# Row maxima split into two float16 parts ahead of their transpose, in a two-layer sliding-window transformer kernel

## The chip, the cores and the metric

The kernel runs on one core of a Trainium2 chip. A core has five engines with a queue each, which work in order and wait for each other through semaphores: TensorE (PE in the profile; its weight loads are shown apart as PEld), VectorE (DVE), ScalarE (ACT), GpSimd (POOL) and SyncE (SP, which issues all DMAs here). The metric is the device time of one execution in microseconds (us), lower is better.

## The reference

Two identical layers over a sequence of 2048 rows of width 640. Each adds to x a causal attention with 32 heads of 20 columns, in which a query sees the 256 latest positions, and then a feed-forward block with a squared ReLU.

```python
def _A_ref(x, wqkv, wo):
    B, S, D = x.shape
    H = 32; Dh = D // H; W = 256
    qkv = (lambda x, *d: x.transpose(*d))((x @ wqkv).reshape(B, S, 3, H, Dh), 2, 0, 3, 1, 4)
    q, k, v = qkv[0], qkv[1], qkv[2]
    scores = jnp.einsum("bhqd,bhkd->bhqk", q, k) * (Dh ** -0.5)
    idx = jnp.arange(S)
    mask = (idx[:, None] - idx[None, :] >= 0) & (idx[:, None] - idx[None, :] < W)
    scores = jnp.where(mask[None, None], scores, -1e9)
    p = _softmax(scores, axis=-1)
    o = jnp.einsum("bhqk,bhkd->bhqd", p, v)
    return (lambda x, *d: x.transpose(*d))(o, 0, 2, 1, 3).reshape(B, S, D) @ wo
...
x = A_x
x = x + _A_ref(_layernorm(x, axis=-1), A_wqkv, A_wo)
x = x + _B_ref(_layernorm(x, axis=-1), B_w1, B_b1, B_w2, B_b2)
x = x + _A_ref(_layernorm(x, axis=-1), A_wqkv, A_wo)
x = x + _B_ref(_layernorm(x, axis=-1), B_w1, B_b1, B_w2, B_b2)
```

The softmax needs, for each query and head, a number near the largest score of its row, to keep the exponentials in range. The change touches how that number travels.

## The kernel before, in words

**Precision.** Dense products (queries, keys, values, output projection, both feed-forward products) are made of float16 halves: each operand is split into a high part and the rest, and three float16 matmuls replace one float32 matmul (function `mm3`, line 256).

**Units.** The sequence is cut into blocks of 256 rows; with two layers there are 16 units. In a unit the 32 heads are taken as 8 quads of four heads, and the quads as four groups G of two (`GQ` = 2). For each quad the program does three things:

- `max_quad`: scores with queries as rows (PE, line 523) into the PSUM tiles `bb`, then eight DVE instructions that add a mask and keep the maximum of each row (line 535; the profile shows each as a main instruction and a read of the accumulator into `mx`). `mx` holds, for one group, 128 partitions (queries) by 16 float32 columns (heads and halves).
- `exp_quad`: the scores once more, now with keys as rows (PE, line 585), the exponentials (ACT, line 598) and the masks (POOL, lines 613 and 617).
- `pv_quad`: exponentials times values (PE, line 647).

**How the maximum enters.** `exp_quad` multiplies 62 rows instead of 60: two extra rows of the query tile `qt` hold the negated row maximum as two float16 parts, and the key tile holds constants there. So the maxima of a group must be turned from a column per head into a row per head. That is `max_out`, once per group, 64 times in the program: a PE transpose of `mx` (line 547) into a PSUM tile `tr`, two DVE operations that make the two float16 parts in the SBUF tile `mT` (lines 552 and 553), and four DMAs that lay the parts into `qt` (line 560). The first `exp_quad` of the group needs them.

**What sets the order.** Each engine's instruction order is written out by the program while it is built. A small planner keeps a simulated time `now` and one clock per engine. PE work is emitted as the Python code reaches it; work for ACT, DVE, POOL and SP is posted as jobs with a cost and a priority (`post`), and `pump` puts a job into its engine's queue when the planner thinks it can start. `need(job)` moves `now` forward until the planner has put that job and believes it finished; it emits nothing on PE meanwhile. `mm_tile` hands out one of two PSUM banks in which dense products, transposes and `pv` results take turns. In units 1 to 15 `together` walks the quads: `exp_quad`, then `max_out` of a group whose maxima were made a turn before, a stretch of dense matmuls, the next `max_quad`, `pv_quad`, more dense matmuls. So a transpose stands in PE's queue right behind the 16 score matmuls of line 585 and ahead of dense matmuls of line 256. On DVE, the work that lies around it is what the planner thought due at that time: the last maxima (535), splits of queries and keys (414), of the feed-forward activations (826) and of layer-norm results (352), and the scaling of attention outputs by reciprocals (726, 729, 736).

Of the kernel before, what the change touches and what calls it, by code (L numbers as in the profile page):

```python
# [10 lines left out]
F32 = mybir.dt.float32  # L11
F16 = mybir.dt.float16
BF16 = mybir.dt.bfloat16
AF = mybir.ActivationFunctionType
ALU = mybir.AluOpType

P = 128
S = 2048
D = 640
# [18 lines left out]
MS = 2.0 ** 4  # L38
# [6 lines left out]
def kernel(ctx: ExitStack, tc: tile.TileContext, x, wqkv, wo, w1, b1, w2, b2, out):  # L45
    nc = tc.nc
# [3 lines left out]
    sb = ctx.enter_context(tc.tile_pool(name="sb", bufs=1))  # L50
    ps = ctx.enter_context(tc.tile_pool(name="ps", bufs=1, space=bass.MemoryType.PSUM))


    ident = sb.tile([P, P], F32, name="ident")
    make_identity(nc, ident)
    neghalf = sb.tile([P, 1], F32, name="neghalf")
    nc.vector.memset(neghalf, -0.5)
    maskb = sb.tile([P, 3 * P], BF16, name="maskb")
# [32 lines left out]
    now, clk, pend, moved = [0.0], {"A": 0.0, "D": 2e3, "G": 0.0, "S": 0.0}, [], [0.0]  # L91
# [28 lines left out]
    def post(eng, cost, fn, *deps, wait=0.0, prio=1, **kw):  # L120

        j = Job(eng, cost, fn, [d for d in deps if d is not None], now[0] + wait, prio, **kw)
        k = len(pend)
        while k and pend[k - 1].prio > prio:
            k -= 1
        pend.insert(k, j)
        return j

    def dma(fn, size, *deps, n=1, cost=450.0, prio=1, **kw):

        return post("S", n * cost, fn, *deps, prio=prio, size=size, **kw)
# [14 lines left out]
    def pass_time():  # L146
        now[0] = max(now[0], min(k.start() for k in pend if k.ready()) - LOOK)
        pump()

    def need(*js):  # L150

        for j in js:
            while j.end is None:
                pass_time()
            now[0] = max(now[0], j.end)
# [4 lines left out]

    banks2 = []

    def mm_tile(shape, name):


        while len(banks2) > 1:
            empty = [b for b in banks2 if b and all(j.end is not None for j in b)]
            if empty:
                b = min(empty, key=lambda b: max(j.end for j in b))
                now[0] = max(now[0], max(j.end for j in b) + LAT)  # L170
                banks2.remove(b)
            else:
                pass_time()
        t = ps.tile(shape, F32, name=name, tag="mm", bufs=2)
        banks2.append([])
        return t, banks2[-1]

# [112 lines left out]
    def split_t(y, dst, job, made, bb=None):  # L290


        need(job)
        for k, (c0, n) in enumerate(((0, 3), (3, 2))):
            if bb is not None:
                tr, jobs = bb[:, k].rearrange("p (c n) -> p c n", n=P), bbjobs
            else:
                tr, jobs = mm_tile([P, 4, P], "tr")
            for c in range(n):
                nc.tensor.transpose(tr[:, c, :], y[:, (c0 + c) * P:(c0 + c + 1) * P], ident)  # L300
            j = post("A", 170 * n, lambda tr=tr, c0=c0, n=n: nc.scalar.copy(dst[:, 0, c0:c0 + n], tr[:, :n]),
                     wait=117 * n, prio=0)
            j = post("D", 170 * n, lambda tr=tr, c0=c0, n=n:
                     nc.vector.tensor_sub(dst[:, 1, c0:c0 + n], tr[:, :n], dst[:, 0, c0:c0 + n]), j, prio=0)  # L304
            jobs.append(j)
            made.append(j)
            yield 117 * n
# [77 lines left out]
    def stage_qk(u, which=(0, 1)):  # L385
# [7 lines left out]
        for j, c0 in order:  # L393
# [11 lines left out]
            dst = kts[u % 3] if j else qts[u]  # L405
            n = min(2, KC - c0)
            acc, jobs = mm_tile([P, 2, T], "acc")
            s = QS / (YS * WS)

# [60 lines left out]
    def stage_v(u, which=range(4)):  # L470
        yT = yTs[u]
        for i in range(2):
            vt = vts[(2 * u + i) % 6][0]
            for h in range(2):
                if 2 * i + h not in which:
                    continue
                acc, jobs = mm_tile([P, 2 * T], "acc")
                need(*[wqj[c] for c in range((2 * D + h * HD) // P, (2 * D + (h + 1) * HD - 1) // P + 1)])
                def out(vt=vt, acc=acc, h=h):
                    nc.scalar.activation(vt[:, h * NP:(h + 1) * NP, 0:DH],  # L480
                                                 acc[:, :HD].rearrange("p (h d) -> p h d", d=DH),
                                                 AF.Copy, scale=1.0 / (YS * WS))

                yield from mm3(acc[:, :HD], lambda a, k: yT[:, a, k, i * P:(i + 1) * P],
                               lambda b, k: wq_s[:, b, k, 2 * D + h * HD:2 * D + (h + 1) * HD], KC, 136,
                               lambda wait: jobs.append(post("A", 320, out, wait=wait, prio=0)))


    GQ = NQ // 4
# [51 lines left out]
    def max_out(u, G):  # L541

        qt, mx = qts[u], mxs.pop((u, G))
        NR = 8 * GQ
        need(*mxjobs.pop((u, G)))
        tr, jobs = mm_tile([P, 4, P], "tr")
        nc.tensor.transpose(tr[:NR, 0, :], mx.rearrange("p e n i -> p (e n i)"), ident)  # L547
        now[0] += 220.0
        mT = sb.tile([NR, 2, P], F16, name="mT", bufs=1)

        def rows():
            nc.vector.tensor_scalar(mT[:, 0], tr[:NR, 0, :], -1.0 / MS, None, op0=ALU.mult)
            nc.vector.scalar_tensor_tensor(mT[:, 1], tr[:NR, 0, :], -1.0 / MS, mT[:, 0],
                                           op0=ALU.mult, op1=ALU.subtract)

        def spread():
            for e in range(2):
                for a in range(2):
                    r = 64 * e + 3 * DH + a
                    nc.sync.dma_start(qt[r:r + 1, 2 * GQ * G:2 * GQ * (G + 1), :].rearrange("p n (i m) -> p (n i) m", i=2),  # L560
                                      mT[4 * GQ * e:4 * GQ * (e + 1), a, :])

        j = post("D", 520, rows, prio=0)
        jobs.append(j)
        rowjobs[u, G] = dma(spread, 16384, j, n=4, cost=600.0, prio=0)

# [341 lines left out]
    def together(ns, ms, dense, cost, share=1.0, whole=True, after=None, pace=0):  # L908
# [5 lines left out]
        for k, (part_, what, m) in enumerate(ts):  # L914
            if what and what[0] == "s":
                quad = exp_quad(what[1])
                for it in late:
                    max_out(*it)
                late.clear()
            if m is not None:  # L920
                max_quad(m)
                if m % GQ == GQ - 1:
                    late.append((m // NQ, m % NQ // GQ))
            if what and what[0] == "v":
                pv_quad(what[1], quad)
            if after and k == 0:
                after()
            part += part_
            while done < cost * share * part / total:
                c = next(dense, None)  # L930
                if c is None:
                    break
                step(c)
                done += c
            if what is None:
                for it in late:
                    max_out(*it)
                late.clear()
# [5 lines left out]
    def flow(todo, dense):  # L944

        todo = list(todo)
        quad = None
        while todo:
            kind, n = todo[0]
            u, G = n // NQ, n % NQ // GQ  # L950
            wants = {"m": [*bbjobs, trips.get((u, 0, n % NQ)), trips.get((u, 1, n % NQ))], "r": mxjobs.get((u, G), [None]),
                     "s": [*bbjobs, *([rowjobs.get((u, G))] if n % GQ == 0 else [])],
                     "v": quad[1][0] if quad else []}[kind]
            if not all(j is not None and j.end is not None and j.end <= now[0] + LOOK for j in wants):
                c = next(dense, None)
                if c is not None:
                    used[0] += c
                    step(c)
                    continue
                need(*[j for j in wants if j is not None])  # L960
            todo.pop(0)
            if kind == "m":
                max_quad(n)
            elif kind == "r":
                max_out(u, G)
            elif kind == "s":
                quad = exp_quad(n)
            else:
                pv_quad(n, quad)
            pump()  # L970
# [29 lines left out]
    for u in range(1, NU):  # L1000
        last = u == NU - 1
        quads, ahead = range(NQ * u, NQ * (u + 1)), range(NQ * u + LEAD, NQ * (u + 1) + LEAD)
        parts, cost, ahead_ln = [], OC + FCST, None
# [49 lines left out]
```

## Time and profile before

| | |
|---|---|
| median of 3 runs | 1659.74 us (1657.5 to 1660.65) |
| span of the profiled execution | 1660.5 us; no other time is given for that execution |
| PE busy | 1595.4 us, 96% |
| DVE, ACT, POOL busy | 1032.8 us, 750.1 us, 636.8 us |
| mean granted TensorE clock | 0.986 |
| transposes of maxima (547) | 64, 280 ns mean each, from 47.8 us to 1553.8 us |
| `mT` operations (552, 553) | 64 each, 279 ns mean each |

How to read the rows. In a timeline a row begins with the start in us from the span's start and the duration; rows that follow each other with the same form are merged with their count; what stands in brackets is the idle time of the engine just before and who ended it. The printed duration of a DVE or PE instruction contains its latency, so the next one often begins a little before the printed end. On PE the starts of neighbouring matmuls tell more than their durations, since matmuls are pipelined. From about 250 us to 1400 us the program repeats itself, apart from the border of the layers near 820 us, with a period of 98.5 us, a unit (the transposes at 622.81 us and 721.27 us are one period apart).

### The profile page before, as it was taken

Reading aid. Unit: us, or ns where it says so; the run is one execution under the profiler, and the core shown is the slowest. Engines: PE = TensorE matmul, PEld = TensorE weight load, DVE = VectorE, ACT = ScalarE, POOL = GpSimd, SP = SyncE. Lnnn points to the kernel's source line nnn. Section 1 sums busy time; section 2 is a strip of 40 time slices with the busy share of each in tenths; the row PEclk is TensorE's granted clock in tenths of the full one; section 3 lists DMA queues with packets and bytes.
Section 4 is the critical chain, followed back from the end, with each engine's and each line's share of the span. In section 5 each row is a group of like instructions: output and inputs, shape, how many; then the busy total and the mean of one; then the engine's idle time right before and its main releaser. Section 6 shows DMA issues by size and latency. Waiting matters only on the chain.

```text
span 1660.5 us, 44547 instructions
## 1 busy us (share of the span) xinstructions
PE 1595.4 (96%) x17574; PEld 1173.0 (71%) x17574; DVE 1032.8 (62%) x3231; ACT 750.1 (45%) x1616; POOL 636.8 (38%) x1309
## 2 busy tenths in 40 slices
PE   7787899999999999999999999999999999999989
PEld 5564676777777777777777777777777777776667
DVE  7566657675665766566565756657665666757341
ACT  4455534535444454544434354444545444453512
POOL 1343533524344353424414243443534344353512
PEclk9897999999999999999999999999999999999999
DMA  8465214343452534335153433424343352421020
GB/s 245 129 179 155 61 61 107 63 118 84 100 101 60 125 69 113 78 102 118 50 136 74 123 82 104 98 68 118 73 109 80 104 115 50 108 70 53 26 64 17
DMA packets 231484, 157.42 MB, mean 95 GB/s; under 512 B 79468, under 2 KB 215020, under 8 KB 231276
## 3 DMA queue, kind: packets, MB, share of 16 engines
q1 hardware_dynamic: 231276, 154.59, 37.8%
q8 instruction: 138, 2.26, 0.6%
q14 instruction: 70, 0.57, 0.1%
HBM read 84.68 MB, written 52.95 MB: 83 GB/s over the span
## 4 chain that ended last, share of the span: by engine, by line
PE 87%; DVE 5%; ACT 3%; DMA 3%; issue 1%; SPq 1%; POOL 0%; DVEq 0%; ACTq 0%; POOLq 0%
PE acc L256 65%; PE pv L647 10%; PE bb L585 6%; PE bb L523 5%; DVE bb L535 2%; ACT pt L598 2%; DMA qk<-qd 1%; PE tr L547 1%; DMA qk<-yl 0%; DMA w_s<-in_A_wqkv_dram 0%; DVE mx L535 0%; DMA ov<-o 0%; DMA qt<-qk 0%; ACT r L816 0%; SPq L560 0%
## 5 line engine op out<-in xcount | busy, mean ns | idle before, releaser
L535 DVE CUSTOM_DVE_ANT_0 bb<-bb,maskb 128x384 f32<-128x384 f32 (+2 forms) x1024 | 510.4, 565 | 117.3 <-PE bb L523 109.4
L598 ACT ACTIVATE pt<-bb 128x512 f32<-128x512 f32 (+1 forms) x736 | 376.5, 602 | 239.9 <-PE bb L585 239.6
L613 POOL TENSOR_SCALAR_AFFINE_SELECT pt<-pt 128x256 f32<-128x256 f32 x448 | 195.0, 440 | 542.8 <-ACT pt L598 521.4
L256 PE MATMUL acc<-y,w_s 128*128 128x256 f16 x2880 | 331.8, 273 | 4.2 <-DVE y L304 1.4
L256 PE MATMUL acc<-w_s,hh 128*128 128x320 f16 x2304 | 326.2, 299 | 0.0
L256 PEld LDWEIGHTS <-w_s 128*128 128x128 f16 x2880 | 278.5, 98 | 58.2 <-issue 25.7
L256 PE MATMUL acc<-yT,wq_s 128*128 128x256 f16 x2400 | 282.7, 276 | 12.6 <-DVE qd L414 10.6
L256 PEld LDWEIGHTS <-hh 128*128 128x128 f16 x2304 | 221.8, 98 | 97.8 <-issue 15.3
L256 PEld LDWEIGHTS <-wq_s 128*128 128x128 f16 x2400 | 233.7, 99 | 58.0 <-issue 27.8
L617 POOL TENSOR_SCALAR_AFFINE_SELECT pt<-pt 128x256 f32<-128x256 f32 x512 | 217.1, 446 | 64.3 <-ACT pt L598 63.2
L826 DVE TENSOR_TENSOR hh<-r,hh 128x256 f16<-128x256 f32 x192 | 91.7, 499 | 208.4 <-ACT hh L823 200.9
L647 PE MATMUL pv<-pt,vt 128*32 128x128 f32 (+1 forms) x3840 | 188.8, 331 | 2.0 <-POOL pt L617 1.4
L820 POOL TENSOR_TENSOR r<-r 128x256 f32<-128x256 f32 x192 | 113.5, 612 | 184.9 <-ACT r L816 183.4
L659 ACT COPY ot<-pv 128x256 f32<-128x256 f32 x128 | 47.6, 372 | 285.6 <-PE pv L647 285.6
L535 DVE DVE_READ_ACCUMULATOR2_ANT mx<- 128x1 f32 x1024 | 142.7, 139 | 0.1
L256 PE MATMUL acc<-wq_s,yT 128*128 128x320 f16 x960 | 142.0, 301 | 0.1
L647 PEld LDWEIGHTS pv<-pt,vt 128*32 128x32 f32 x3840 | 104.2, 110 | 49.1 <-issue 17.6
L256 PE MATMUL acc<-wo_s,od 128*128 128x320 f16 x900 | 131.9, 301 | 3.6 <-DVE x L758 1.7
L816 ACT ACTIVATE r<-acc,b1s 128x256 f32<-128x256 f32 x192 | 80.6, 471 | 99.8 <-PE acc L256 98.4
L256 PEld LDWEIGHTS <-yT 128*128 128x128 f16 x960 | 93.0, 98 | 40.4 <-issue 7.0
L585 PE MATMUL bb<-qt,kt 62*128 62x128 f16 (+1 forms) x1920 | 109.4, 246 | 10.6 <-DVE mx L535 9.8
L256 PEld LDWEIGHTS <-od 128*128 128x128 f16 x900 | 86.1, 98 | 45.9 <-issue 11.1
(84 smaller groups left out, 1175.7 us busy)
## 6 DMA issues: line engine op xcount, KB each, us to landing
qt<-qk SPq DMA_DIRECT2D x30, 480.0 KB
kt<-qk SPq DMA_DIRECT2D x30, 480.0 KB
qk<-qd SPq DMA_DIRECT2D x17, 640.0 KB
o<-ot SPq DMA_DIRECT2D x256, 42.0 KB
od<-o SPq DMA_DIRECT2D x13, 640.0 KB
qk<-yl SPq DMA_DIRECT2D x13, 640.0 KB
qk<-qd SPq DMA_DIRECT2D x17, 320.0 KB
xt<-in_A_x_dram SPq DMA_DIRECT2D x16, 320.0 KB
```

Source lines behind the costliest of these rows:

```text
L256: nc.tensor.matmul(acc, lhs(a, c), rhs(b, c), start=(k == 0), stop=(k == 3 * nk - 1))
L523: nc.tensor.matmul(to, qt[r, p, i * P:(i + 1) * P], kt[r, p, a:b], start=True, stop=True)
L535: nc.vector.tensor_tensor_reduce(out=v, in0=v, in1=mask, scale=1.0, scalar=-3.0e38, op0=ALU.add, op1=ALU.max, accum_out=accum)))
L585: nc.tensor.matmul(bb[e][:, k, o:o + w], kt[r, 2 * qd + j, ko:ko + P], qt[r, 2 * qd + j, q0 * P:q0 * P + w], start=True, stop=True)
L598: nc.scalar.activation(box["pt"][:, :o], bb[e][:, k, :o], AF.Exp, scale=SCALE / (QS * QS))
L613: nc.gpsimd.affine_select(out=m, in_=m, pattern=[[0, 2], [-1, P]], compare_op=ALU.is_gt, fill=0.0, base=0, channel_multiplier=1)
L617: nc.gpsimd.affine_select(out=m, in_=m, pattern=[[0, 2], [1, P]], compare_op=ALU.is_ge, fill=0.0, base=0, channel_multiplier=-1)
L647: nc.tensor.matmul(pv[32 * jj:32 * (jj + 1), q0 * P:(q0 + qn) * P], vf[:, c:c + 32], pj[:, j, :], start=(k == 0), stop=(k == len(steps) - ...
L659: nc.scalar.copy(ot[:, qd % 2], pv)
L816: nc.scalar.activation(box["r"], acc[:, f, :], AF.Relu, bias=b1s[:, f0 + f:f0 + f + 1], scale=1.0 / (YS * WS))
L820: nc.gpsimd.tensor_tensor(box["r"], box["r"], box["r"], op=ALU.mult)
L826: nc.vector.tensor_sub(hh[:, 1, f, :], box["r"], hh[:, 0, f, :])
```

## The change

The two float16 parts are now made from `mx` itself, on 128 partitions by 16 columns, ahead of the transpose. Both parts lie side by side in a new float16 tile `mh` of 32 columns; one float16 transpose (with a float16 identity, made once at the start) turns all 32 columns into 32 rows, and one DVE copy takes them from PSUM to `mT`. The four DMAs are the same, with other source rows. The parts are posted as a DVE job, and the code waits for it with `need` ahead of the transpose.

```diff
@@ -53,6 +53,8 @@
     ident = sb.tile([P, P], F32, name="ident")
     make_identity(nc, ident)
+    ident16 = sb.tile([P, P], F16, name="ident16")
+    nc.vector.tensor_copy(ident16, ident)
...
-    def mm_tile(shape, name):
+    def mm_tile(shape, name, dtype=F32):
...
-        t = ps.tile(shape, F32, name=name, tag="mm", bufs=2)
+        t = ps.tile(shape, dtype, name=name, tag="mm", bufs=2)
...
         need(*mxjobs.pop((u, G)))
-        tr, jobs = mm_tile([P, 4, P], "tr")
-        nc.tensor.transpose(tr[:NR, 0, :], mx.rearrange("p e n i -> p (e n i)"), ident)
-        now[0] += 220.0
-        mT = sb.tile([NR, 2, P], F16, name="mT", bufs=1)
+        mh = sb.tile([P, 2, NR], F16, name="mh", bufs=1)
+        flat = mx.rearrange("p e n i -> p (e n i)")
+
+        def parts():
+            nc.vector.tensor_scalar(mh[:, 0], flat, -1.0 / MS, None, op0=ALU.mult)
+            nc.vector.scalar_tensor_tensor(mh[:, 1], flat, -1.0 / MS, mh[:, 0], op0=ALU.mult, op1=ALU.subtract)
+
+        need(post("D", 200, parts, prio=0))
+        tr, jobs = mm_tile([P, 8 * P], "tr", F16)
+        nc.tensor.transpose(tr[:2 * NR, :P], mh.rearrange("p a n -> p (a n)"), ident16)
+        now[0] += 60.0
+        mT = sb.tile([2 * NR, P], F16, name="mT", bufs=1)
 
         def rows():
-            nc.vector.tensor_scalar(mT[:, 0], tr[:NR, 0, :], -1.0 / MS, None, op0=ALU.mult)
-            nc.vector.scalar_tensor_tensor(mT[:, 1], tr[:NR, 0, :], -1.0 / MS, mT[:, 0],
-                                           op0=ALU.mult, op1=ALU.subtract)
+            nc.vector.tensor_copy(mT, tr[:2 * NR, :P])
...
-                                      mT[4 * GQ * e:4 * GQ * (e + 1), a, :])
+                                      mT[NR * a + 4 * GQ * e:NR * a + 4 * GQ * (e + 1), :])
...
-        j = post("D", 520, rows, prio=0)
+        j = post("D", 200, rows, prio=0)
```

Because jobs are put by the planner's clocks, the order on the engines moves a little too. The line numbers of the changed program are higher by 2 from line 56 on and by 8 behind `max_out` (354 there is 352 here, 416 is 414, 537 is 535, 737 is 729, 861 is 853).

The first place is on DVE, around the 29th of the 64 transposes (721 us in the profile before). Line 352 makes the low parts of a layer-norm result, line 853 adds a feed-forward product to x. Before:

```order
L535 ISA mx 128x1
L853 SCALAR_TENSOR_TENSOR x_9224<-acc,x_9224 128x320 [waits PE_49]
L352 TENSOR_TENSOR yl<-xt,yl 128x640 [waits Activation_49] x2
L552 TENSOR_SCALAR mT<-tr 16x128 [waits DMAHW4_49,DMAHW3_49,PE_49]
L553 SCALAR_TENSOR_TENSOR mT<-tr,mT 16x128 [waits DVE_49]
L853 SCALAR_TENSOR_TENSOR x_9225<-acc,x_9225 128x320 [waits PE_49]
```

In the changed program:

```order
L537 ISA mx 128x1
L861 SCALAR_TENSOR_TENSOR x_9276<-acc,x_9276 128x320 [waits PE_49]
L354 TENSOR_TENSOR yl<-xt,yl 128x640 [waits Activation_49] x2
L552 TENSOR_SCALAR mh<-mx 128x16 [waits DVE_49]
L553 SCALAR_TENSOR_TENSOR mh<-mx,mh 128x16 [waits DVE_49]
L562 COPY mT<-tr 32x128 [waits DMAHW4_49,DMAHW3_49,PE_49]
L861 SCALAR_TENSOR_TENSOR x_9277<-acc,x_9277 128x320 [waits PE_49]
```

The parts stand where the two `mT` operations stood, behind the same instructions, and the copy stands right behind them. On PE, at the same place, the transpose was one instruction and is now a weight load that waits for DVE, and a matmul:

```order
L593 LDWEIGHTS kt_79
L593 MATMUL bb<-qt,kt_79 128x256
L557 LDWEIGHTS mh [waits DVE_49]
L557 MATMUL tr<-ident_66,mh 32x128
L258 LDWEIGHTS hh
L258 MATMUL acc<-w_s,hh 128x320
```

It stands between the same neighbours as before, the last score matmul and the first dense one.

The second place is DVE around the next transpose (746 us before), where attention outputs are scaled: line 729 multiplies, 726 makes the reciprocals, 736 makes low parts. Before:

```order
L414 SCALAR_TENSOR_TENSOR qd<-acc,qd 128x256 [waits Activation_49]
L729 TENSOR_TENSOR od<-od,rs 128x5x64 [waits DMAHW1_49]
L726 RECIPROCAL rs<-rs 128x64
L552 TENSOR_SCALAR mT<-tr 16x128 [waits DMAHW7_49,DMAHW2_49,PE_49]
L553 SCALAR_TENSOR_TENSOR mT<-tr,mT 16x128 [waits DVE_49]
L736 TENSOR_TENSOR od<-od 128x5x64 [waits Activation_49]
```

In the changed program:

```order
L416 SCALAR_TENSOR_TENSOR qd<-acc,qd 128x256 [waits Activation_49]
L737 TENSOR_TENSOR od<-od,rs 128x5x64 [waits DMAHW1_49]
L552 TENSOR_SCALAR mh<-mx 128x16 [waits DVE_49]
L553 SCALAR_TENSOR_TENSOR mh<-mx,mh 128x16 [waits DVE_49]
L744 TENSOR_TENSOR od<-od 128x5x64 [waits Activation_49]
L562 COPY mT<-tr 32x128 [waits DMAHW7_49,DMAHW2_49,PE_49]
L734 RECIPROCAL rs<-rs 128x64
```

Here the parts have moved ahead of one reciprocal, which is now behind the copy.

The third place is in the first unit, around the 5th transpose (120 us before), where DVE also makes low parts of the feed-forward weights (line 196, 198 in the changed program). Before:

```order
L535 ISA mx 128x1
L196 SCALAR_TENSOR_TENSOR w_s<-w_s 128x5x128
L286 TENSOR_SCALAR xt<-xt,bmv 128x640 [waits Pool_49]
L552 TENSOR_SCALAR mT<-tr 16x128 [waits DMAHW6_49,DMAHW7_49,DMAHW0_49,PE_49]
L553 SCALAR_TENSOR_TENSOR mT<-tr,mT 16x128 [waits DVE_49]
```

In the changed program:

```order
L537 ISA mx 128x1
L198 SCALAR_TENSOR_TENSOR w_s<-w_s 128x5x128
L198 SCALAR_TENSOR_TENSOR w_s<-w_s 128x5x128 [waits DMAHW3_49,Activation_49]
L552 TENSOR_SCALAR mh<-mx 128x16 [waits DVE_49]
L553 SCALAR_TENSOR_TENSOR mh<-mx,mh 128x16 [waits DVE_49]
L562 COPY mT<-tr 32x128 [waits DMAHW6_49,DMAHW7_49,DMAHW0_49,PE_49]
L288 TENSOR_SCALAR xt<-xt,bmv 128x640 [waits Pool_49]
```

A second weight split, which stood later before, has come in ahead of the parts, and the layer-norm scaling of line 286 has gone behind the copy.

## The prediction

> **What bounds the kernel now.** I read the page's shares and its chain of waits first, then busy time by stage, then the rows of the transpose and its two followers, and last the timeline around single transposes.
>
> ```profile
> span 1660.5 us, 44547 instructions
> PE 87%; DVE 5%; ACT 3%; DMA 3%; issue 1%; SPq 1%; POOL 0%; DVEq 0%; ACTq 0%; POOLq 0%
> ```
>
> ```profile
> core 0: us, PE busy (x) PEld busy (x) DVE busy (x) ACT busy (x) POOL busy (x), PEclk, DMA share, GB/s
> 0.00:190.00 190.00, 147.28 (x1386) 103.50 (x1390) 120.51 (x391) 97.45 (x191) 63.14 (x107) 0.89 0.61 167
> 190.00:800.00 610.00, 606.07 (x6959) 450.37 (x6948) 393.84 (x1217) 282.06 (x612) 248.73 (x527) 1.00 0.38 89
> 1000.00:1400.00 400.00, 399.44 (x4586) 296.19 (x4582) 263.54 (x812) 183.74 (x395) 158.22 (x336) 1.00 0.39 93
> ```
>
> PE bounds it. In the first 190 us PE lacks 42.7 us of busy time; in the repeating stretches it lacks 3.9 of 610 us and 0.6 of 400 us. So a new wait of PE there has nothing to hide in: it lengthens the program by its full size. DVE, at 394 of 610 us, has room, but the question is when it is free, not how much it does.
>
> ```profile
> L547 PEld LDWEIGHTS tr<-ident,mx x64: 86/87/90, 47.8 to 1553.8; 128*16 128x16 f32 x64
> L547 PE MATMUL tr<-ident,mx x64: 269/277/383, 47.8 to 1553.8; 128*16 128x128 f32 x64
> L552 DVE TENSOR_SCALAR mT<-tr x64: 269/279/281, 48.1 to 1554.1; 16x128 f16<-16x128 f32 x64
>   PE tr L547: 24.4, 49
> ```
>
> These rows of the tile `tr` and its users show the present direction: DVE sits idle for PE's transpose (49 times, 24.4 us), PE hardly ever for DVE. After the change PE must wait for DVE in the middle of its queue.
>
> **The change part by part.** The new wait is PE's weight load of `mh`. Ahead of it PE has the 16 score matmuls, behind it the dense ones and everything else of PE; ACT, POOL and DVE wait for those in turn. How long it lasts: DVE reaches the parts when the instruction ahead of them in its queue is done (E, its printed end), then needs two small operations. I compare E with the start of the present transpose (S), for each of the 64, by the new DVE order. One example of each kind that repeats:
>
> ```profile
> 719.93 1.55 DVE L352 TENSOR_TENSOR yl<-xt,yl 128x640 f16<-128x640 f32 x2
> 721.27 0.28 PE L547 MATMUL tr<-ident,mx 128*16 128x128 f32 x1
> 721.39 0.30 PE L256 MATMUL acc<-w_s,hh 128*128 128x320 f16 x1
> ...
> 744.55 0.42 DVE L414 SCALAR_TENSOR_TENSOR qd<-acc,qd 128x256 f16<-128x256 f32 x1
> 744.89 0.48 DVE L729 TENSOR_TENSOR od<-od,rs 128x320 f32<-128x320 f32 x1
> 745.71 0.28 PE L547 MATMUL tr<-ident,mx 128*16 128x128 f32 x1
> ...
> 769.87 0.69 DVE L414 SCALAR_TENSOR_TENSOR yl<-acc,yl 128x512 f16<-128x512 f32 x1
> 770.65 0.28 PE L547 MATMUL tr<-ident,mx 128*16 128x128 f32 x1
> ...
> 793.90 0.99 DVE L826 TENSOR_TENSOR hh<-r,hh 128x256 f16<-128x256 f32 x2 [0.46 <-ACT hh L823]
> 795.01 0.28 PE L547 MATMUL tr<-ident,mx 128*16 128x128 f32 x1
> ```
>
> S minus E is -0.21 us behind line 352, +0.34 behind 729 (the reciprocal that stood there has moved back), +0.09 behind 414 and +0.11 behind 826. The first and the last of the ten places of the first kind agree to 0.01 us:
>
> ```profile
> 326.06 1.55 DVE L352 TENSOR_TENSOR yl<-xt,yl 128x640 f16<-128x640 f32 x2
> 327.40 0.28 PE L547 MATMUL tr<-ident,mx 128*16 128x128 f32 x1
> ...
> 1399.15 1.55 DVE L352 TENSOR_TENSOR yl<-xt,yl 128x640 f16<-128x640 f32 x2
> 1400.49 0.28 PE L547 MATMUL tr<-ident,mx 128*16 128x128 f32 x1
> ```
>
> The price of the two small operations, 128 partitions by 16 columns from SBUF, has no row of its own. The nearest:
>
> ```profile
> L278 DVE TENSOR_SCALAR bmv<-bmv 128x1 f32<-128x1 f32 x64 | 9.9, 154 | 2.2
> L286 DVE TENSOR_SCALAR xt<-xt,bmv 128x640 f32<-128x640 f32 x32 | 19.9, 622 | 10.3 <-POOL bmv L284 9.5
> L196 DVE SCALAR_TENSOR_TENSOR wq_s<-w_s,wq_s 128x640 f16<-128x640 f32 x12 | 9.2, 818 | 1.8 <-ACT wq_s L194 1.8
> ```
>
> Between 1 and 640 columns line 278 and 286 give 154 + 15 x (622 - 154) / 639 = 165 ns for the first; 278 and 196 give 170 ns for the second, which waits for the first. Lower bound 154 ns each, upper bound the 279 ns of the PSUM operation at line 552; I take 165 and 170, since 16 columns is far nearer to 1 than to 640.
>
> [...]
>
> Around them: an independent DVE instruction starts 0.08 us before the printed end of the one ahead (744.55 + 0.42 against 744.89); one that needs its predecessor starts 0.03 us after its end, and PE 0.05 us after a DVE end:
>
> ```profile
> 710.86 0.19 DVE L277 BATCH_NORM_AGGREGATE bmv<-bst 128x2 f32<-128x12 f32 x1
> 711.08 0.15 DVE L278 TENSOR_SCALAR bmv<-bmv 128x1 f32<-128x1 f32 x1
> ...
> 70.04 0.69 DVE L414 SCALAR_TENSOR_TENSOR qd<-acc,qd 128x512 f16<-128x512 f32 x1 [9.65 <-ACT qd L411]
> 70.78 1.44 PE L256 MATMUL acc<-yT,wq_s 128*128 128x256 f16 x6 [10.57 <-DVE qd L414]
> ```
>
> So the transpose can start at E - 0.08 + 0.165 + 0.03 + 0.17 + 0.05 = E + 0.34, and PE loses 0.34 - (S - E) where that is positive:
>
> - behind line 352, 10 places: 0.55 each, 5.5 us
> - behind 414 (`yl`), 12 places: 0.25 each, 3.0 us
> - behind 826, 13 places: 0.24 mostly, 3.4 us
> - behind 729, 10 places: nothing
> - the other 17 that are not of the two below: 1.7 us, most of them nothing because DVE was done 0.4 us or more earlier.
>
> Two places in the first unit are of their own kind. At 59.94 us PE already waits 10.57 us right behind the transpose for line 414 (last fence); the parts now stand behind that same instruction, so the wait moves ahead of the transpose and grows by 0.34 us only. At 120 us a second weight split has come in ahead of the parts:
>
> ```profile
> 119.31 1.92 DVE L196 SCALAR_TENSOR_TENSOR w_s<-w_s 128x640 f16<-128x640 f32 x1
> 120.22 0.38 PE L547 MATMUL tr<-ident,mx 128*16 128x128 f32 x1
> ...
> L196 DVE SCALAR_TENSOR_TENSOR w_s<-w_s 128x640 f16<-128x640 f32 x4 | 4.9, 1244 | 0.0
> ```
>
> The first split ends at 121.2; the second takes up to 1.24 us, so E is about 122.2 and the transpose starts 2.3 us later than now.
>
> What PE gains: the weight load is the same size of work; the moving side becomes float16.
>
> ```profile
> L523 PE MATMUL bb<-kt,qt 60*128 60x128 f16 x1472 | 99.0, 220 | 4.5 <-ACT pt L598 4.3
> L523 PE MATMUL bb<-kt,qt 60*128 60x256 f16 x704 | 73.3, 272 | 0.0
> ```
>
> 128 float16 columns more cost 52 ns. The present transpose holds PE for 0.12 us (721.27 to 721.39). So at most 0.06 us is saved, at least nothing; I take 0.05, or 3.2 us over 64.
>
> [...]
>
> On DVE, 2 x 279 ns go, 165 + 170 ns and a copy of 32 x 128 come; the copy lies between 154 and 279 ns. That is within 0.06 us per group of what was there, on an engine 62% busy. DVE idles about 0.3 us ahead of the copy, as it did ahead of `mT`; behind it DVE is, counted from PE's transpose, about 0.3 us earlier than now, so no later wait on DVE gets worse. The float16 identity is one 128x128 copy while DVE waits for the first rows of x. The four DMAs start when the copy ends, about when both old operations had ended; the group's `exp_quad` is a turn or more away, and no row of PE's waits names them.
>
> Sum: 5.5 + 3.0 + 3.4 + 1.7 + 0.3 + 2.3 - 3.2 = **13.0 us**. Against the span of 1660.5 that is 1673.5; the runs' median lies 0.8 us lower, so about 1673 us, 0.8% slower. With the parts at 154 ns each every late place loses 0.03 less, about 1 us; with 279 ns each, 0.22 us more at about 35 late places and 0.22 at the ten behind 729, about 10 us more.
>
> **The rivals.**
>
> *The small operations are dear* (279 ns each, or PE resumes later than 0.05 us behind a DVE semaphore when it is a weight load that waits): about 1683 us. For it: lines 196 and 286 vary with what POOL does (1244 against 818 ns). Against: 154 ns is the mean of 64 at one column.
>
> *The stalls are partly bought back.* A free transpose pays 7.7 us instead of 3.2, and the first unit loses nothing: 13.0 - 4.5 - 2.6 = 6 us, 1666 us. Against: the pitch of float16 columns.
>
> *The first unit is rearranged to the better.* PE lacks 42.7 us there, 10.57 of them in one wait whose origin is a DMA (ACT's 411 waits for the query write). The planner now puts five dense matmuls, some exponentials and weight loads elsewhere. If that removed the 10.57 us wait and three more, beyond 13.0 us in all, the change would not be slower: removing 17 us gives 1656 us. It decides from 13 of the 42.7 us. Against: the parts at 60 us stand behind the very instruction that PE waits for, and the DMA queue ahead of it is ordered as before.
>
> *The change does not do what it says*: PE does not wait because the planner has set the parts early. The new order shows them early at one kind of place only (729); otherwise they stand where `mT` stood. If all places were like it, the time would be 1660.5 - 3.2, less the 0.8 us: 1656.5 us.
>
> **How the numbers follow.** Forecast 73%, dear operations 12%, partly bought back 8%, the first unit better 5%, no wait 2%. This kernel's time can be told from no change to about 0.2%, 3.3 us. Faster: 5%, from the last two; same: 7%, the rest of these and the lower end of the partly bought back case; slower: 88%. The range for 8 in 10 goes from 1664 (the partly bought back case and 2 us for the first unit) to 1686 (dear operations with a little more in the first unit).
>
> **What would show it.** In the profile after: PE's weight load of `mh` waiting for the parts, some 35 times or more and 12 to 16 us in total, with 0.5 us behind line 354 and a quarter behind 416 and the activations' split; small operations near 165 ns; the transpose holding PE for about 0.06 us; DVE's wait for `tr` still there, ahead of the copy; PE's missing time in 190 to 800 us grown from 3.9 to about 9 us. I am wrong if those waits are absent, or if the first unit differs by more than 5 us.

## The result and the profile after

The changed kernel takes 1686.58 us (median of 4 runs, 1685.31 to 1688.24) against 1659.74: 1.62% slower, ratio 1.0162 with a 95% interval of 1.0148 to 1.0176. The forecast was 1673 us with a range of 1664 to 1686: the sign was right, the size half of what came, and the time lies 0.6 us above the range. The profiled execution has a span of 1685.5 us, 25.0 more than before.

The page of the changed kernel: span, PE and DVE, and the chain of waits.

```profile
span 1685.5 us, 44536 instructions
PE 1603.0 (95%) x17574; PEld 1174.9 (70%) x17574; DVE 1036.3 (61%) x3296; ACT 752.4 (45%) x1616; POOL 629.5 (37%) x1309
PE 66%; DVE 13%; ACT 9%; POOL 7%; DMA 3%; issue 2%; SPq 1%; POOLq 0%; ACTq 0%; DVEq 0%
```

PE's share of the chain has gone from 87% to 66% and DVE's from 5% to 13%. The busy time by stage, in the columns of the prediction's second fence (start:end, length, PE, PEld, DVE, ACT and POOL busy, clock, DMA share, GB/s):

```profile
0.00:190.00 190.00, 138.57 (x1285) 96.82 (x1286) 123.00 (x398) 91.62 (x179) 58.02 (x94) 0.87 0.61 167
190.00:800.00 610.00, 602.24 (x6867) 444.82 (x6866) 387.02 (x1218) 278.12 (x599) 238.66 (x513) 1.00 0.36 88
```

Two readings. In the first 190 us PE is busy 8.7 us less than before (147.28 then). In the repeating stretch it lacks 7.8 of 610 us where it lacked 3.9. The waits of PE, over the whole program (waited for: us in total, times, longest):

```profile
PE tr L557 <- DVE mh L553: 16.2, 42, 2.9
PE tr L557 <- ACT pt L606: 11.9, 1, 11.9
PE acc L258 <- ACT stg L741: 10.5, 2, 5.7
```

The first row is the new wait. The second is the old wait of 10.57 us at 60 us, now ahead of the transpose as forecast; the row names line 606, but the transpose (at 70.61 us) starts 53 ns behind the end of the parts, so it is the parts that it waited for. The third is in the first unit, where the kernel before waited 4.1 us for the same cast (its line 733). Now the transpose and its neighbours:

```profile
L552 DVE TENSOR_SCALAR mh<-mx x64: 110/168/559, 46.1 to 1578.4; 128x16 f16<-128x16 f32 x64
L553 DVE SCALAR_TENSOR_TENSOR mh<-mx,mh x64: 174/176/536, 46.3 to 1579.0; 128x16 f16<-128x16 f32 x64
L557 PE MATMUL tr<-ident,mh x64: 229/229/288, 46.5 to 1579.6; 128*32 128x128 f16 x64
L562 DVE COPY mT<-tr x64: 203/211/213, 46.8 to 1579.9; 32x128 f16<-32x128 f16 x64
```

And the timeline of the changed kernel around the transpose that stood at 721.27 us, behind the layer-norm's low part (line 352, now 354):

```profile
735.19 1.55 DVE L354 TENSOR_TENSOR yl<-xt,yl 128x640 f16<-128x640 f32 x2
735.76 0.83 PE L593 MATMUL bb<-qt,kt 62*128 62x256 f16 x16
736.66 0.17 DVE L552 TENSOR_SCALAR mh<-mx 128x16 f16<-128x16 f32 x1
736.86 0.18 DVE L553 SCALAR_TENSOR_TENSOR mh<-mx,mh 128x16 f16<-128x16 f32 x1
737.09 0.23 PE L557 MATMUL tr<-ident,mh 128*32 128x128 f16 x1 [0.49 <-DVE mh L553]
737.25 0.79 PEld L258 LDWEIGHTS <-hh 128*128 128x128 f16 x7
737.25 0.99 PE L258 MATMUL acc<-w_s,hh 128*128 128x320 f16 x6
```

Line 354 ends at 736.74 and the transpose starts at 737.09, 0.35 us behind (forecast: 0.34). But the next dense matmul follows 0.16 us behind the transpose (0.12 before), and its weight load, which before started with the transpose (2 ns behind it in the median of all), now starts with that matmul (158 ns behind the transpose). So the "faster" transpose holds PE longer:

```profile
721.27 0.28 PE L547 MATMUL tr<-ident,mx 128*16 128x128 f32 x1
721.27 0.89 PEld L256 LDWEIGHTS <-hh 128*128 128x128 f16 x7
721.39 0.98 PE L256 MATMUL acc<-w_s,hh 128*128 128x320 f16 x6
```

(This fence is the kernel before.) To the nanosecond the step from transpose to dense matmul is 114 ns before and 162 ns after, in the median of all of them.

In the first unit most of the time is lost in one stretch, between the sixth and the seventh transpose. The kernel before, then the changed one:

```profile
144.21 0.28 PE L547 MATMUL tr<-ident,mx 128*16 128x128 f32 x1
184.50 0.28 PE L547 MATMUL tr<-ident,mx 128*16 128x128 f32 x1
```

```profile
142.68 0.23 PE L557 MATMUL tr<-ident,mh 128*32 128x128 f16 x1 [0.46 <-DVE mh L553]
191.85 0.23 PE L557 MATMUL tr<-ident,mh 128*32 128x128 f16 x1
```

40.29 us have become 49.17: 8.9 us. PE's waits in 140 to 192 us, before and after:

```profile
PE acc L256 <- ACT stg L733: 4.1, 1, 4.1
PE tr L300 <- DVE xt L286: 3.1, 1, 3.1
PE acc L256 <- DVE stg L736: 2.9, 2, 2.1
```

```profile
PE acc L258 <- ACT stg L741: 10.5, 2, 5.7
PE tr L302 <- DVE xt L288: 6.9, 1, 6.9
```

These waits were 10.1 us and are 17.4; all of PE's idle time between the two transposes was 11.7 us and is 19.2. The granted clock in 140 to 192 us fell as well, from 0.84 to 0.77 (in the first 190 us it is 0.89 before, 0.87 in the changed kernel and 0.87 in run 2 below); whether that makes the other 1.3 of the 8.9 us is not shown. What PE waits for longest in total are the float16 casts of the attention output on ACT, and the last of them, 5.7 us, is the wait that is new. In ACT's queue of the changed kernel this cast stands behind six exponentials and four weight conversions. The multiplication on DVE that feeds it is late too, but done at 163.3 us, 3.9 us before the cast starts:

```profile
162.83 0.48 DVE L737 TENSOR_TENSOR kt<-kt,rs 128x320 f32<-128x320 f32 x1
161.80 3.04 ACT L606 ACTIVATE pt<-bb 128x512 f32<-128x512 f32 x6 [3.89 <-PE bb L593]
164.67 1.40 ACT L196 ACTIVATE w_s<-stg 128x640 f16<-128x640 f32 x2
165.93 1.40 ACT L200 ACTIVATE stg<-stg 128x640 f32<-128x640 f32 x2
167.18 0.49 ACT L741 CAST stg<-kt 128x320 f16<-128x320 f32 x1
```

In the kernel before, the multiplication started at 155.65 us and the cast at 160.26, ahead of the weight conversions.

**Theories.** The trace gives three causes that lie on top of each other: the waits for the parts, a longer hold of PE by the transpose, and a new order in the first unit. The main theory is that all three count and add up. Its rivals: that the order is harmless and the loss in the first unit comes from the transposes' own waits there; and that the hold is only the wait seen twice, or belongs to float16, or to the transpose instruction, or to the 32 columns of its weights.

### The profile page after: what moved, and what is told of

It reads as the page before. It is cut to its first block, busy times and chain, and to the rows that moved or that the text cites. A ratio compares the mean times of both kernels' runs of the same rounds, so it can differ in the third digit from the quotient of the medians.

```text
span 1685.5 us, 44536 instructions
## 1 busy us (share of the span) xinstructions
PE 1603.0 (95%) x17574; PEld 1174.9 (70%) x17574; DVE 1036.3 (61%) x3296; ACT 752.4 (45%) x1616; POOL 629.5 (37%) x1309
## 4 chain that ended last, share of the span: by engine, by line
PE 66%; DVE 13%; ACT 9%; POOL 7%; DMA 3%; issue 2%; SPq 1%; POOLq 0%; ACTq 0%; DVEq 0%
PE acc L258 49%; PE pv L655 8%; DVE bb L537 7%; ACT pt L606 5%; PE bb L525 4%; PE bb L593 3%; POOL x L786 2%; POOL r L828 2%; POOL pt L625 1%; DMA xt<-in_B_b_dram 1%; DVE mx L537 1%; DVE yl L416 1%; DMA qk<-qd 1%; DVE yl L354 1%; ACT r L824 1%
## 5 line engine op out<-in xcount | busy, mean ns | idle before, releaser
L621 POOL TENSOR_SCALAR_AFFINE_SELECT pt<-pt 128x256 f32<-128x256 f32 x448 | 187.5, 422 | 578.3 <-ACT pt L606 562.6
L625 POOL TENSOR_SCALAR_AFFINE_SELECT pt<-pt 128x256 f32<-128x256 f32 x512 | 216.4, 444 | 60.9 <-ACT pt L606 59.7
L655 PE MATMUL pv<-pt,vt 128*32 128x128 f32 (+1 forms) x3840 | 192.5, 332 | 1.5 <-POOL pt L625 1.0
L537 DVE DVE_READ_ACCUMULATOR2_ANT mx<- 128x1 f32 x1024 | 146.1, 143 | 0.0
```

The lines of the kernel that those rows point to most:

```text
L537: nc.vector.tensor_tensor_reduce(out=v, in0=v, in1=mask, scale=1.0, scalar=-3.0e38, op0=ALU.add, op1=ALU.max, accum_out=accum)))
L621: nc.gpsimd.affine_select(out=m, in_=m, pattern=[[0, 2], [-1, P]], compare_op=ALU.is_gt, fill=0.0, base=0, channel_multiplier=1)
L625: nc.gpsimd.affine_select(out=m, in_=m, pattern=[[0, 2], [1, P]], compare_op=ALU.is_ge, fill=0.0, base=0, channel_multiplier=-1)
L655: nc.tensor.matmul(pv[32 * jj:32 * (jj + 1), q0 * P:(q0 + qn) * P], vf[:, c:c + 32], pj[:, j, :], start=(k == 0), stop=(k == len(steps) - ...
```

## The experiments

All times are medians; "the kernel before" is the one run beside each of them on the same chip (1660.0 to 1661.5 us), and ratios are against that.

**1. The new work in the old order.** The parts are issued where the transpose is emitted, and the planner's durations keep their old values, so that every other instruction of every engine stands where it stood before.

```
-        need(post("D", 200, parts, prio=0))
+        parts()
...
-        now[0] += 60.0
+        now[0] += 220.0
...
-        j = post("D", 200, rows, prio=0)
+        j = post("D", 520, rows, prio=0)
```

> The changed work in the order of before: the parts are put on DVE at once in max_out, and the planner's numbers (220 behind the transpose, 520 for the followers) are those of before, so that all other instructions of all engines stand in the order of before. Theory A (three causes: PE waits for the parts, some 14 us; the transpose holds PE 0.162 us instead of 0.114, 64 times, 3 us; the new order of the first unit, some 8 us, now absent): about 1677 us, at the 6th to 7th transposes no jump of 8.9 us. Rival B (the order is innocent; the waits and what they push about in the first unit cost all): as the changed kernel, 1686 us, with that jump.

Measured: 1674.72 us, ratio 1.0086 (1.0064 to 1.0108). Busy time by stage of this run:

```profile
0.00:190.00 190.00, 146.69 (x1394) 103.19 (x1395) 122.30 (x401) 97.59 (x191) 63.82 (x107) 0.89 0.60 167
190.00:800.00 610.00, 602.34 (x6898) 445.78 (x6888) 389.01 (x1238) 278.48 (x602) 240.83 (x517) 1.00 0.37 89
```

In the first stage PE's busy time is back within 0.6 us of the kernel before, and PE's waits between the sixth and the seventh transpose are the old ones (4.1 us for line 741); in the repeating stretch PE is as little busy as in the changed kernel. So the order costs about 12 of the 27 us, and the waits and the hold the other 14 (11 to 18 by the interval; the four times of this run lie 10 us apart). Most of the 12 is lost in the first unit: at the tenth transpose this run is level with the kernel before (251.63 and 251.60 us), where the changed kernel is 9.6 us late. From there to the last transpose it loses 13.4 us and the changed kernel 16.2, so some 3 us of the order's price fall into the later units.

**2. The old work in the new order.** The kernel before, with the old transpose and its two operations, but with the durations that the changed kernel tells the planner and an empty job where it posts the parts.

```
+        need(post("D", 200, lambda: None, prio=0))
...
-        now[0] += 220.0
+        now[0] += 60.0
...
-        j = post("D", 520, rows, prio=0)
+        j = post("D", 200, rows, prio=0)
```

> The instructions of before (float32 transpose of mx, two operations on DVE behind it) in the order of the changed kernel: an empty job takes the planner's time of the parts, and the planner's numbers are those of the change. Theory A: the first unit's new order alone costs 8 to 9 us, so about 1668 us, with the repeating part as before. Rival B: within 2 us of before, 1660 us.

Measured: 1670.81 us, ratio 1.0063 (1.0049 to 1.0076): 10 us slower with no new work at all. Its two largest waits of PE in 140 to 192 us are those of the changed kernel, to the tenth:

```profile
PE acc L256 <- ACT stg L734: 10.5, 2, 5.7
PE tr L300 <- DVE xt L286: 6.9, 1, 6.9
```

With run 1 this settles the first unit: the order alone makes the jump, and neither the parts nor the float16 transpose is needed for it. 14 and 10 us add up to 24 of the 27; the intervals of the two runs are wide enough for the rest.

**3. The parts early.** The order of before, and the two small operations right behind the last maximum of their group, so that they are done when PE comes to nearly every transpose.

```
+                    if last:
+                        make_parts(u, G, mx)
...
-        need(post("D", 200, parts, prio=0))
+        mh = mhs.pop((u, G))
```

(`make_parts` holds the two operations of `parts`; the planner's durations are as in run 1.)

> The order of before, and the two operations that make the parts stand on DVE right behind the last maximum of the group, long ahead of the transpose, so that PE has nothing to wait for. Theory A: only the longer hold of the float16 transpose is left, 64 x 0.05 = 3 us, so about 1663 us. Rival C (the hold of 0.162 us is an effect of the wait, and goes with it): 0.06 us hold, 3 us less than before, 1657 us.

Measured: 1662.28 us, ratio 1.0013 (1.0004 to 1.0023). The same work in the same order as run 1 but for the place of two operations is 12.4 us faster: that is the price of the waits for the parts, less what takes their place. PE's rows for the transpose show that something does:

```profile
PE tr L562 <- DVE yl L416: 2.7, 12, 0.4
PE tr L562 <- DVE mh L553: 2.1, 4, 0.8
```

Behind line 416 the two small operations, now ahead of it, make that line itself late (it ends at 768.48 us, the transpose starts at 768.54), so at these 12 places PE waits for it instead; the second row is what is left of the 15.5 us that run 1 waits for the parts. The timeline around the transpose behind line 354:

```profile
717.83 1.55 DVE L354 TENSOR_TENSOR yl<-xt,yl 128x640 f16<-128x640 f32 x2
718.76 0.23 PE L562 MATMUL tr<-ident,mh 128*32 128x128 f16 x1
718.93 1.26 PE L258 MATMUL acc<-w_s,hh 128*128 128x320 f16 x8
```

The transpose starts while line 354 still runs, with no wait for the parts, which were done 1.25 us earlier; and the dense matmul still comes 162 ns behind it. So the hold is not the wait seen twice.

**4. The transpose in float32 again**, of the changed kernel, with the parts in float32. The first part is then the whole value and the second is zero, so that the low rows that the scores receive are left out.

```
-        mh = sb.tile([P, 2, NR], F16, name="mh", bufs=1)
+        mh = sb.tile([P, 2, NR], F32, name="mh", bufs=1)
...
-        tr, jobs = mm_tile([P, 8 * P], "tr", F16)
-        nc.tensor.transpose(tr[:2 * NR, :P], mh.rearrange("p a n -> p (a n)"), ident16)
+        tr, jobs = mm_tile([P, 4 * P], "tr")
+        nc.tensor.transpose(tr[:2 * NR, :P], mh.rearrange("p a n -> p (a n)"), ident)
```

> As the changed kernel, but the parts and the transpose are float32 and the copy makes float16 of them; what is left out is the second part of the maxima (it becomes zero, since the first is no longer rounded). Theory A: the float32 transpose holds PE 0.114 us, as in before, so some 3 us less than the changed kernel, 1683 us, with the same waits. Rival D (the longer hold comes from 32 columns instead of 16 or from the wait, not from float16): 0.16 us hold and 1686 us.

Measured: 1686.47 us, ratio 1.0161 (1.0146 to 1.0177): nothing gained. Behind line 354 the hold is indeed down to 0.12 us, and the next weight load starts with the transpose, though its weights have 32 columns here too:

```profile
737.64 0.28 PE L557 MATMUL tr<-ident,mh 128*32 128x128 f32 x1 [0.49 <-DVE mh L553]
737.64 0.63 PEld L258 LDWEIGHTS <-hh 128*128 128x128 f16 x5
737.76 0.71 PE L258 MATMUL acc<-w_s,hh 128*128 128x320 f16 x4
```

At most other waiting places the float32 transpose starts 0.146 us behind the parts' end, where the float16 one needs 0.054, and the hold is 0.108 us. Wait and hold together are then 0.254 against 0.216 us, so what the hold gives the start takes back; the last transpose of this run comes 1.1 us earlier than in the changed kernel. The forecast of 1683 us missed that; the run does show that 32 columns alone do not make the long hold: it takes float16 as well.

**5. An ordinary matmul instead of the transpose instruction**, in the kernel of run 3: a float16 matmul against the identity, into float32 PSUM.

```
-        tr, jobs = mm_tile([P, 8 * P], "tr", F16)
-        nc.tensor.transpose(tr[:2 * NR, :P], mh.rearrange("p a n -> p (a n)"), ident16)
+        tr, jobs = mm_tile([P, 4 * P], "tr")
+        nc.tensor.matmul(tr[:2 * NR, :P], mh.rearrange("p a n -> p (a n)"), ident16, start=True, stop=True)
```

> The order of before, the parts right behind the last maximum of their group, as in the run that put the parts early (1662.3 us, next dense matmul 162 ns behind the transpose), but the 128x32 block is turned by an ordinary float16 matmul against the identity into float32 PSUM instead of by the transpose instruction. Theory T (the transpose instruction is what keeps the next weight load from being fetched ahead): the next dense matmul starts 60 to 115 ns behind it, 64 x 0.05 to 0.10 = 3 to 6 us less: 1656 to 1659 us. Theory W (it is the 32 columns of the weight load that do it, a size that no other matmul ahead of a dense one has): still about 160 ns and 1662 us. Theory N (neither; every change of the weights' kind costs this): 160 ns here and in the run with 128 columns too.

Measured: 1662.61 us, ratio 1.0018 (1.0010 to 1.0027), and the step from the transpose to the dense matmul is 162 ns as in run 3. It is not the transpose instruction. (What was expected calls 32 columns a size that no other matmul ahead of a dense one has. That holds for float16 only: the `pv` matmuls of line 655 load 32 columns in float32 and stand ahead of dense ones too.)

**6. 128 columns of weights**, in the kernel of run 3: the two parts lie in a zeroed buffer of 128 x 128, and all of it is loaded and turned.

```
+    mh128 = sb.tile([P, 8, 8 * GQ], F16, name="mh")
+    nc.vector.memset(mh128, 0.0)
...
-        mhs[u, G] = mh = sb.tile([P, 2, 8 * GQ], F16, name="mh", bufs=1)
+        mhs[u, G] = mh = mh128
...
-        nc.tensor.transpose(tr[:2 * NR, :P], mh.rearrange("p a n -> p (a n)"), ident16)
+        nc.tensor.transpose(tr[:, :P], mh.rearrange("p a n -> p (a n)"), ident16)
```

> As the run that put the parts early (1662.3 us, 162 ns), but the two parts lie in a zeroed buffer of 128 x 128, and the transpose loads all 128 columns of it and turns them, the last 96 of them zeros that nobody reads. Theory W (the 32-column weight load is what keeps the next load from being fetched ahead): the next dense matmul starts 60 to 115 ns behind the transpose, 3 to 6 us less: 1656 to 1659 us. Theory T (the transpose instruction does it): still about 160 ns and 1662 us. Theory N: as T.

Measured: 1657.86 us, ratio 0.9988 (0.9979 to 0.9997), 4.4 us below run 3 and the only kernel of the study that is faster than the one before, by an interval that just leaves out 1. The place behind line 354 once more:

```profile
718.56 0.10 PEld L564 LDWEIGHTS <-mh 128*128 128x128 f16 x1 [0.21 <-DVE yl L354]
718.56 0.23 PE L564 MATMUL tr<-ident,mh 128*128 128x128 f16 x1
718.57 0.97 PEld L258 LDWEIGHTS <-hh 128*128 128x128 f16 x8
718.63 1.11 PE L258 MATMUL acc<-w_s,hh 128*128 128x320 f16 x7
```

Four times as many weights, and PE is free again after 67 ns instead of 162; the next weight load starts 11 ns behind the transpose. That is 0.096 us per transpose, 6.1 us over 64; in the repeating part the transposes of this run draw ahead of those of run 3 by 0.10 us each. The medians differ by less, 4.4 us; part of that is the first unit, which takes 0.7 us longer in this run's profile than in that of run 3 (first to tenth transpose).

**7. The attention output's scaling first, in the first unit only**, in the changed kernel: the jobs behind lines 737 to 744 get the most urgent priority there.

```
-            j = post("D", 575, ratio, loaded, prio=2)
-            j = post("D", 409, times, j, prio=2)
-            j = post("A", 360, high, j, prio=0 if i < 2 else 2)
-            js.append(post("D", 402, low, j, prio=2))
+            p0 = 0 if u == 0 else 2
+            j = post("D", 575, ratio, loaded, prio=p0)
+            j = post("D", 409, times, j, prio=p0)
+            j = post("A", 360, high, j, prio=0 if i < 2 else p0)
+            js.append(post("D", 402, low, j, prio=p0))
```

> The changed kernel with one number changed for the first unit alone: the scaling of the attention output (ratio, multiplication, the float16 cast on ACT, the rest on DVE) is given the most urgent priority in the planner, so that its fourth cast and multiplication come ahead of the exponentials, the maxima and the weight conversions that stood ahead of them. Theory Q (the planner's new order in the first unit, with the cast of line 741 and what is late behind it, costs the 8.9 us between the sixth and the seventh transpose): the jump there shrinks to 0 to 4 us and the time to 1678 to 1683 us. Theory R (the loss there comes from the transposes' own waits, not from that order): the jump stays near 8.9 and the time near 1686 us. If the priority moves the wait to the exponentials or to the weight conversions instead, the jump stays and the row that PE waits for there is another one than line 741's.

Measured: 1680.47 us, ratio 1.0127 (1.0111 to 1.0142), 6.1 us below the changed kernel. The sixth and the seventh transpose stand 41.96 us apart (40.29 before, 49.17 in the changed kernel), and the wait for line 741 is gone:

```profile
141.20 0.23 PE L557 MATMUL tr<-ident,mh 128*32 128x128 f16 x1 [0.46 <-DVE mh L553]
183.16 0.23 PE L557 MATMUL tr<-ident,mh 128*32 128x128 f16 x1
```

```profile
PE tr L302 <- DVE yT L306: 6.5, 2, 6.0
PE tr L302 <- DVE xt L288: 5.9, 1, 5.9
```

The first of these two rows is a wait that has taken its place, earlier (at 152 us); most of the gain was kept all the same, since the stretch as a whole is 7.2 us shorter. The wait for the layer norm (line 288), 3.1 us in the kernel before and 6.9 in the changed one, is still 5.9, so where that one comes from stays open.

**8. Both together**: run 7 with the 128 columns of run 6 (the waits for the parts stay).

```
+    mh128 = sb.tile([P, 8, 8 * GQ], F16, name="mh")
+    nc.vector.memset(mh128, 0.0)
...
-        mh = sb.tile([P, 2, NR], F16, name="mh", bufs=1)
+        mh = mh128
...
-        nc.tensor.transpose(tr[:2 * NR, :P], mh.rearrange("p a n -> p (a n)"), ident16)
+        nc.tensor.transpose(tr[:, :P], mh.rearrange("p a n -> p (a n)"), ident16)
```

> The changed kernel with the scaling of the first unit put ahead (1680.5 us) and the parts in the zeroed 128 x 128 buffer, so that the transpose loads 128 columns of weights: the order of all instructions is that of the run with the scaling put ahead. Theory W with waits (the hold and the waits add up): the next dense matmul starts about 66 ns behind the transpose here too, 64 x 0.096 = 6.1 us less: 1674 us, and the waits of the weight load for the parts, about 14 us, stay. That would be 14 us above the kernel before, for the waits alone. Rival V (where PE has just waited for the parts, the next weight load finds no time to be fetched ahead, so the hold stays at 162 ns in the 35 places that wait): 64 - 35 = 29 places x 0.096 = 2.8 us less: 1677.7 us.

Measured: 1673.10 us, ratio 1.0071 (1.0055 to 1.0088), where 1674 was expected for costs that add and 1677.7 if the hold stayed at the waiting places. A waiting place:

```profile
728.91 0.23 PE L559 MATMUL tr<-ident,mh 128*128 128x128 f16 x1 [0.49 <-DVE mh L555]
728.92 0.29 PEld L258 LDWEIGHTS <-hh 128*128 128x128 f16 x3
728.98 0.43 PE L258 MATMUL acc<-w_s,hh 128*128 128x320 f16 x2
```

The wait of 0.49 us is there as in the changed kernel, and the hold is 68 ns. What is left, 11.6 us above the kernel before, is mostly the waits, but it is near the 12.4 us of runs 1 and 3 partly by chance: the hold is now 46 ns shorter than in the kernel before, 3 us over 64, and some of the new order's price is still there.

## Why the prediction was right in sign and wrong in size

**The waits: right, place by place.** Forecast was a start at E + 0.34 us; the changed kernel shows 0.345 to 0.350 at the waiting places. The extra gap ahead of the transpose, from the start of the last score matmul and against the 200 ns without a wait, is 0.56 us behind 354 (forecast 0.55), 0.25 behind 416 (0.25), 0.25 behind line 834 (0.24) and 0.01 behind 737 (0). The parts take 168 and 176 ns (165 and 170). The 42 waits of the first row are the forecast "some 35 or more", and their 16.2 us lie just above the forecast 12 to 16. PE's missing time in 190 to 800 us is 7.8 us (about 9 was forecast). The rivals "dear small operations" and "no wait" fall with that; the first came out near the measured time by luck, for a reason that was not there.

**The step "What PE gains": wrong in sign, 6.3 us.** I took 0.05 us saved per transpose, -3.2 us, and bounded it by 0 and 0.06. Measured is 0.048 us lost, 64 x 0.048 = +3.1 us. The bound "at least nothing" rested on the moving side's pitch (52 ns for 128 float16 columns) and on "the weight load is the same size of work" (its recorded length is 87 ns before and 92 ns after). It left out what the trace showed and I had not read: that the next weight load starts 2 ns behind the float32 transpose. With 32 float16 columns it starts 158 ns behind it, and the dense matmul with it. Run 6 shows the size of the error from the other side: with 128 columns the hold is 66 ns, and 64 x (0.114 - 0.066) = 3.1 us would have been the gain that I forecast.

**The first unit: 6.5 us too little.** Forecast there were 0.34 us at 60 us, 2.3 at 120 us and nothing else, with 10 x 0.05 off: 2.1 us up to the tenth transpose. That one comes 9.6 us later than before (251.60 and 261.21 us); of the 7.5 us between, 1.0 is the hold and 6.5 the order. Run 2, which has the order alone, is 6.3 us late there. The step that failed is that I costed only the transposes in the first unit, and took the moved weight split at 120 us for the whole of the new order. That place came out at 0.1 us, since PE reached it 3 us earlier and waited 2.89 us there. What mattered most is 40 us later and has nothing to do with a transpose: a cast on ACT that is late behind a late multiplication, six exponentials and four weight conversions (run 2 shows it with the old work, run 7 without that wait). My rival about the first unit had the mechanism, that the planner puts exponentials and weight loads elsewhere, with the opposite sign and 5%. I wrote that I would be wrong if that unit differed by more than 5 us, and it did.

**The sum, mended.** From the tenth transpose to the last the shift grows from 9.6 to 25.8 us: 16.2. The forecast for these 54 was 5.5 + 3.0 + 3.4 + 1.7 - 54 x 0.05 = 10.9; with the measured +0.048 in place of the -0.05 it is 16.2. With 9.6 from the first ten that makes the 25.8 us seen at the last transpose. That it fits to the tenth is partly luck: the gaps ahead of these 54 transposes grow by 14.4 us and not by 13.6, and small terms that I did not have take the difference back.

Two of them nearly cancel in each unit. In the kernel before, a dense matmul 0.96 us behind the transpose of the 826 kind waits 0.3 us for the second `mT` operation (at 697.50 us), and the shorter copy ends that: in run 1 the step from there to the next transpose, the one behind 354, grows by 0.32 us, where wait and hold alone would make 0.61. In the new order an attention matmul in the same step waits 0.25 us for POOL, so in the changed kernel it grows by 0.58; run 2 shows this wait too (0.25 us between the same two transposes).

**What the last lever is worth.** The kernel of run 6 differs from the changed one in three ways, each measured: the order of before (12 us), the parts ahead of the other DVE work (12.4 us) and 128 columns (4.4 us). It is 0.12% below the kernel before (0.03 to 0.21%), about what this measurement can tell. So in this kernel the idea of the change pays for itself only with all three, and then hardly.

## What to carry to other kernels

When a planner or list scheduler sets the order, a change of one job's duration or dependence reorders work that has nothing to do with it. Price that separately, above all where the bound engine already has idle time: run the old work in the new order. For a small matmul between large ones, read when the next weight load starts, not how long the matmul lasts; if it starts behind instead of with it, try the small matmul with more columns of weights and read again: here 32 float16 columns padded to 128 took the step to the next matmul from 162 to 66 ns (runs 3 and 6), 4.4 us in the medians.

## What the hardware showed that was not expected

The step from the transpose of a 128-row block to the next dense matmul, with nothing to wait for and at the full clock (1.00 granted from 190 to 800 us): float32 with 16 columns of weights 114 ns; float32 with 32 columns 122 to 123 (108 behind most waits for the parts); float16 with 32 columns 162, as a transpose or as an ordinary matmul (and as much behind a wait for the parts); float16 with 128 columns 66. The recorded length of the float16 weight load hardly differs (92 ns for 32 columns, 96 for 128); what differs is when the next load starts, 158 ns behind the transpose with 32 columns and 11 ns with 128. Why 32 float16 columns hold the next load back and 32 float32 columns do not stays open; no run has a width between 32 and 128.

The transpose of the changed kernel, in float16, starts 54 ns behind the end of the parts where it waits for them, while the float32 transpose of run 4 starts 146 ns behind it at most places and 55 ns behind it where line 354 stands ahead; why the two differ stays open. That gave back in run 4 nearly all that its shorter hold had gained.
